# Eleven products of 128 rows for twelve of 112 in the projections of an attention kernel

## The chip, the cores and the metric

The kernel runs on one core of a Trainium2 chip. The metric is the device time of one execution in microseconds. A core has a matrix engine (PE, with its weight load PEld), three engines for vector work (DVE, ACT, POOL), a queue engine (SP) that here issues most of the transfers, and 16 DMA engines.

## What is computed

The output is the concatenation of two independent parts, each of 2048 rows by 448 columns, in fp32.

```
# part A: a state-space convolution, per feature
dt = exp(log_dt); A = -exp(log_A_real) + 1j*A_imag; C = (C_real + 1j*C_imag)*dt[:,None]
K = 2*einsum("dn,dnl->dl", C, exp((A*dt[:,None])[:,:,None]*arange(L))).real
a = irfft(rfft(u_t, 2L) * rfft(K, 2L))[..., :L] transposed + u * D_skip
# part B: attention with 16 heads of 28 features
q, k, v = split(x @ wqkv)               # x: 2048 x 448, wqkv: 448 x 1344
p = softmax(q k^T * 28**-0.5)
b = (p v) @ wo
```

The change touches the product x @ wqkv alone.

## The kernel before

The kernel runs in two stages. The first, about 190 us of the profiled execution, computes q, k and v and stores them in DRAM. Beside it, it builds the starting values ("seeds") of the state-space kernel for eight groups of features, in tiles called tri, sg, qhat and x_e, which end in the DRAM tensors sd. Then follow the row maxima of the first unit of attention, and from about 232 us on the main loop: 16 units of 16 steps with scores, exponentials and p v, in whose gaps the work of part A is placed.

In the first stage x comes in four blocks of 512 rows (c = 0 to 3, load_x). `transposes` (L464) turns a block into four slices of features by 512 rows with PE and splits each slice into a high part xh, rounded to fp32r by ACT, and the remainder xl, which DVE subtracts. The weights are split in the same way when the kernel starts: w_g with i = 0 and 1 (kept in the tile khat until the keys need it) for q and k, and vh and vl for v. A product of full precision is then taken as three products in fp32r, xh with the high weights, xh with the remainder of the weights, and xl with the high weights. Four slices of CK = 112 features make twelve products that accumulate in one PSUM tile:

```
for k in range(NCK):
    for i, x_ in ((0, xh), (1, xh), (0, xl)):
        nc.tensor.matmul(pp, w_g[:, i, s, k, g]..., x_[k], start=n == 0, stop=n == 3 * NCK - 1)
```

`qk_proj` (L474) is such a job for one block, for q or k (s = 0 or 1) and for one group of four heads, with 512 columns; `v_proj` (L509) one for 128 rows of v, with 448 columns. A block has eight jobs of the first kind and four of the second; in the last block the v jobs come first. The PSUM tiles of the jobs (pm) come from a ring of three banks. Each job ends in an evacuation by ACT and DVE (the tiles hl, vst, in the last block xn), and for keys also in kb and dhl, from where SP stores the results.

The weights come in through `wns`, four tiles of 112 rows. x blocks lie in xn, tiles of 512 columns of which 448 are used.

Around the change the order of the instructions is not written by hand: in this stage a scheduler in the build orders each engine's instructions by its own estimate of when they can start, from the program order of the jobs and of the seeds' slots (PW, SP and SH set how these are interleaved). The seeds' steps on ACT alone hold a fixed order among themselves. From the main loop on, instructions are kept in program order. All instructions are recorded by one helper, so that the profile gives line 75 for nearly all of them, and groups are told apart by their tiles.

Of the kernel before, what the change touches and what calls it, by code (L numbers as in the profile page):

```python
# [8 lines left out]
F32 = mybir.dt.float32  # L9
F32R = mybir.dt.float32r  # L10
I32 = mybir.dt.int32
AF = mybir.ActivationFunctionType
ALU = mybir.AluOpType
# [5 lines left out]
D = 448  # L19

H = 16
DH = 28
G = 4
HG = H // G
CQ = 512
NQ = L // CQ
NK = L // 128
CK = 112
NCK = D // CK
SCALE = DH ** -0.5  # L30
NU = G * NQ
NS = NU * NK
# [9 lines left out]
SGB, XB, XL = 2, 5, 4  # L42
# [48 lines left out]
def body(ctx, tc, a, out):  # L91
    nc = Engines(tc)
    nc.kept = KEPT["p"]
    x, wqkv, wo, u_a = a["B_x"][0], a["B_wqkv"], a["B_wo"], a["A_u"][0]
    out = out[0]

    def pool(stack, name, bufs=1, space=None, side=None):
        kw = {} if space is None else {"space": space}
        if side:
            kw["side"] = side  # L100
        return stack.enter_context(tc.tile_pool(name=name, bufs=bufs, reuse_waits="tile", **kw))
# [23 lines left out]
    def w_tile():  # L125

        n_ring[0] += 1
        return ps_w[0].tile([128, CQ], F32, name=f"pm{n_ring[0] % ps_w[1]}")
# [5 lines left out]
    k0_t = k0_p.tile([128, HG, L], F32R, name="khat")  # L134
# [91 lines left out]
    with ExitStack() as st:  # L226
# [3 lines left out]
        x_p = pool(xst, "x_p")  # L230
        y_p = pool(wst, "y_p", side="right")
        ps_w[0] = pool(st, "ps_w", 1, PSUM)
        ps_t = pool(st, "ps_t", 2, PSUM)
# [3 lines left out]
        xns = {}  # L237

        def load_x(c):
            xs = x[c * CQ:(c + 1) * CQ, :].rearrange("(t p) d -> p t d", p=128)  # L240
            for h in range(2):
                xns[c, h] = y_p.tile([128, 2, CQ], F32, name="xn", bufs=3)[:, :, :D]
                nc.sync.dma_start(xns[c, h], xs[:, 2 * h:2 * h + 2, :])

        first = lambda o: (o // 4) * DF + (o % 4) * (JF // 4)
        nats = {}
# [43 lines left out]
        def turn_dt():  # L290
            dt_ps = ps_t.tile([128, CQ], F32, name="pt")[:PO, :NO]
            nc.tensor.transpose(dt_ps, dt_o, ident[:NO, :NO])
            for i, f in enumerate((1.0, 0.15915494309189535, 2.0, -2.0, -1.0)):
                nc.vector.tensor_scalar(dt_all[:, i, :], dt_ps, f, None, op0=ALU.mult)

        load_x(0)
        w_g = k0_t[:CK].rearrange("p g (i s k h e) -> p i s k g h e", i=2, s=2, k=NCK, h=HG)
        vh = y_p.tile([CK, NCK, D], F32R, name="vh")
        vl = y_p.tile([CK, NCK, D], F32R, name="vl")
        nc.gpsimd.memset(k0_t[:CK].rearrange("p g (n e) -> p (g n) e", e=32)[:, :, DH:].bitcast(F32), 0.0)  # L300
        vst = [x_p.tile([128, H, 32], F32, name=f"vst{i}") for i in range(2)]
        for t in vst:
            nc.gpsimd.memset(t[:, :, DH:DH + 1], 1.0)
# [1 line left out]
        wns = []  # L305
        for i in range(2):
            wn = t_p.tile([128, 3, LV, BO * 16], F32, name="tri", bufs=2).rearrange("p t k h -> p (t k h)")
            wn = wn[:CK, :2 * 3 * D].rearrange("p (k s d) -> p k s d", k=2, s=3)
            wns += [wn[:, 0], wn[:, 1]]
        for k in range(NCK):  # L310
            nc.sync.dma_start(wns[k], wqkv[k * CK:(k + 1) * CK, :].rearrange("p (s d) -> p s d", s=3))
        pw2 = s_p.tile([128, LV], F32, name="pw2")
        nc.sync.dma_start(pw2, a["pw2"])
        nc.sync.dma_start(kones, a["kones"])
# [1 line left out]
        nc.sync.dma_start(w1, a["w1"])  # L316
        for k in range(NCK):
            for s in (1, 0):
# [143 lines left out]
        xh, xl = {}, {}  # L462

        def transposes(c):  # L464
            for k in range(NCK):
                pt = ps_t.tile([128, CQ], F32, name="pt")[:CK]
                for t in range(4):
                    nc.tensor.transpose(pt[:, t * 128:(t + 1) * 128], xns[c, t // 2][:, t % 2, k * CK:(k + 1) * CK], ident)
                xh[k] = x_p.tile([CK, CQ], F32R, name="xh", bufs=XB)
                xl[k] = x_p.tile([CK, CQ], F32R, name="xl", bufs=XL)  # L470
                nc.scalar.activation(xh[k], pt, AF.Copy)
                nc.vector.tensor_tensor(xl[k], pt, xh[k].bitcast(F32), ALU.subtract)

        def qk_proj(c, s, g):  # L474
            pp = w_tile()
            n = 0
            for k in range(NCK):
                for i, x_ in ((0, xh), (1, xh), (0, xl)):
                    nc.tensor.matmul(pp, w_g[:, i, s, k, g].rearrange("p h e -> p (h e)"), x_[k],
                                     start=n == 0, stop=n == 3 * NCK - 1)  # L480
                    n += 1

            def evac():
                if c == NQ - 1 and s == 0:
                    hl = y_p.tile([128, 2, CQ], F32, name="xn", bufs=3).bitcast(F32R)
                else:
                    hl = x_p.tile([128, 2, CQ], F32R, name="hl", bufs=3)
                th, tl = hl[:, 0], hl[:, 1]
                if s == 1:
                    nc.scalar.activation(th, pp, AF.Identity, bias=kones)  # L490
                    nc.vector.scalar_tensor_tensor(tl, pp, kones, th.bitcast(F32), op0=ALU.add, op1=ALU.subtract)
                else:
                    nc.scalar.activation(th, pp, AF.Copy)
                    nc.vector.tensor_tensor(tl, pp, th.bitcast(F32), ALU.subtract)
                if s == 1 and c < 2:
                    HC = CQ // 2
                    kb = y_p.tile([128, HC], F32, name="kb")
                    dhl = y_p.tile([128, 2, HC], F32R, name="dhl")
                    dh, dl = dhl[:, 0], dhl[:, 1]
                    nc.scalar.activation(kb, pp[:, HC:], AF.Copy)  # L500
                    nc.vector.tensor_tensor(kb, pp[:, :HC], kb, ALU.subtract)
                    nc.scalar.activation(dh, kb, AF.Copy)
                    nc.gpsimd.tensor_tensor(dl, kb, dh.bitcast(F32), ALU.subtract)
                    nc.sync.dma_start(kd_d[g][:, :, c * HC:(c + 1) * HC].rearrange("i p l -> p i l"), dhl.bitcast(F32))
                nc.sync.dma_start((k_d[g][:, :, c * CQ:(c + 1) * CQ] if s == 1 else q_d[g][c]).rearrange("i p l -> p i l"),
                                  hl.bitcast(F32))
            return evac

        def v_proj(c, t):  # L509
            pp = w_tile()  # L510
            n = 0
            ts = slice(t * 128, (t + 1) * 128)
            for k in range(NCK):
                for w_, x_ in ((vh, xh), (vl, xh), (vh, xl)):
                    nc.tensor.matmul(pp[:, :D], x_[k][:, ts], w_[:, k, :], start=n == 0, stop=n == 3 * NCK - 1)
                    n += 1

            def evac():
                vs = vst[t % 2]
                nc.scalar.activation(vs[:, :, :DH], pp[:, :D].rearrange("p (h e) -> p h e", e=DH), AF.Copy)  # L520
                nc.sync.dma_start(v_d[c][:, :, t], vs.rearrange("p (g h) e -> p g (h e)", g=G))
            return evac

        work = []
        for c in range(NQ):
            jobs = [lambda c=c, s=s, g=g: qk_proj(c, s, g) for g in range(G) for s in (1, 0)]
            v_jobs = [lambda c=c, t=t: v_proj(c, t) for t in range(4)]
            jobs = v_jobs + jobs if c == NQ - 1 else jobs + v_jobs
            jobs[0] = (lambda c, f: lambda: (transposes(c), f())[1])(c, jobs[0])
            if c + 1 < NQ:  # L530
                jobs[1] = (lambda c, f: lambda: (load_x(c + 1), f())[1])(c, jobs[1])
            work += jobs
# [572 lines left out]
    s = NS  # L1105
# [63 lines left out]
```

## Time and profile before

| what | us |
|---|---|
| median of three runs | 1278.88 |
| these runs | 1276.07 to 1279.31 |
| the profiled execution | 1278.37 |
| its span, first to last instruction | 1276.6 |
| PE busy in the span | 1223.9 |
| ACT busy | 967.5 |
| DVE busy | 923.0 |
| POOL busy | 846.2 |

The span is the time between the first and the last instruction on the core; the time of the execution also holds what lies around it. A busy PE is not a PE at its peak, since the ends of its pipelined products are modelled; the distance between the starts of two products tells its pace. Stretches of the stage are given in microseconds from the start of the span.

### The profile page before, as it was taken

What the parts mean: (1) busy time and instruction counts of PE and PEld (TensorE: products, weight loads), DVE (VectorE), ACT (ScalarE), POOL (GpSimd) and SP (SyncE); (2) the same over time, 40 slices, a digit from 0 to 9 for tenths busy, and PEclk for the clock granted to TensorE, in tenths of its full rate; (3) what the DMA queues carried; (4) which work ended last, traced back from release to release, by engine and by line L of the source; (5) the groups of instructions that cost most, each with busy time, mean ns of one, the idle gap of its engine ahead of it and who ended that gap; (6) DMA issues with size and microseconds to landing.
All of it is one profiled execution on the core that took longest, in us unless ns stands there. A gap on an engine that the chain in (4) does not pass through costs nothing.

```text
span 1276.6 us, 33328 instructions
## 1 busy us (share of the span) xinstructions
PE 1223.9 (96%) x12641; PEld 699.3 (55%) x12641; DVE 923.0 (72%) x2106; ACT 967.5 (76%) x2162; POOL 846.2 (66%) x728
## 2 busy tenths in 40 slices
PE   7789887999999999999999999999999999999997
PEld 5667664555555555555555555555555545544433
DVE  6788866877777877877788888888897645645111
ACT  6878765788888888888878888888887666656452
POOL 2666750897788888878599999989995222324321
PEclk9889999899999999999999999999999999999999
DMA  7768699446564645375633133422324533657666
GB/s 216 244 223 288 233 304 346 113 93 186 160 149 113 168 119 168 113 235 167 176 94 104 49 88 97 154 81 71 88 54 156 179 131 135 204 170 228 198 170 167
DMA packets 200089, 205.36 MB, mean 161 GB/s; under 512 B 95992, under 2 KB 158520, under 8 KB 197880
## 3 DMA queue, kind: packets, MB, share of 16 engines
q1 hardware_dynamic: 199400, 202.63, 52.6%
q8 instruction: 100, 1.64, 0.5%
q10 hardware_dynamic: 528, 0.59, 0.2%
q14 instruction: 61, 0.50, 0.1%
HBM read 120.73 MB, written 82.18 MB: 159 GB/s over the span
## 4 chain that ended last, share of the span: by engine, by line
PE 75%; DVE 8%; POOL 6%; ACT 4%; issue 3%; DMA 3%; SPq 0%; ACTq 0%; POOLq 0%; DVEq 0%
PE pm L75 43%; PE pss L75 16%; PE po L75 16%; POOL e L75 2%; DVE tri L75 1%; ACT rl L75 1%; POOL qhat L75 1%; DVE mx L75 1%; DVE sg L75 1%; POOL eu L75 1%; ACT tri L75 1%; DVE px L75 1%; DVE qhat L75 1%; DVE hl L75 1%; DMA sd<-qhat 1%
## 5 line engine op out<-in xcount | busy, mean ns | idle before, releaser
L75 ACT ACTIVATE p<-pss 128x512 f32<-128x512 f32 x1024 | 561.0, 610 | 112.5 <-PE pss L75 107.2
L75 PE MATMUL pss<-qhat,khat 128*128 128x512 f32 x1024 | 403.2, 400 | 1.5 <-ACT p L75 1.4
L75 DVE TENSOR_REDUCE mx<-pm 128x1 f32<-128x512 f32 x480 | 308.6, 684 | 109.1 <-PE pm L75 107.2
L75 PE MATMUL pm<-khat,qhat 128*128 128x512 f32 x749 | 325.9, 438 | 6.4 <-ACT rl L75 4.2
L75 POOL TENSOR_TENSOR e<-e,sdb 128x256 f32<-128x256 f32 x168 | 201.8, 1201 | 110.6 <-ACT e L75 101.2
L75 PE MATMUL po<-p,v 128*32 128x512 f32 x2048 | 269.1, 594 | 0.0
L75 POOL TENSOR_TENSOR e<-e,eu 128x256 f32<-128x256 f32 x168 | 248.2, 1477 | 13.2
L75 PEld LDWEIGHTS pm<-khat,qhat 128*128 128x128 f32 x749 | 141.0, 189 | 201.9 <-ACT p L75 47.8
L75 DVE CUSTOM_DVE_ANT_0 rl<-pm,rl 128x512 f32<-128x512 f32 x259 | 178.3, 689 | 72.1 <-ACT rl L75 69.1
L75 PEld LDWEIGHTS pss<-qhat,khat 128*128 128x128 f32 x1024 | 190.6, 189 | 46.7 <-issue 10.8
L75 POOL TENSOR_TENSOR eu<-e,sdb 128x256 f32<-128x256 f32 x168 | 201.9, 1202 | 0.0
L75 POOL TENSOR_TENSOR p<-pr,pr 64x448 f32<-64x448 f32 x64 | 73.2, 1144 | 158.2 <-PE pm L75 132.8
L75 ACT ACTIVATE rl<-pm 128x512 f32<-128x512 f32 x259 | 156.6, 606 | 14.0 <-PE pm L75 8.4
L75 DVE TENSOR_TENSOR g<-g,zg 128x128 f32<-128x128 f32 x392 | 162.2, 414 | 3.4
L75 PE MATMUL pm<-kdif,qhat 128*128 128x512 f32 x249 | 100.5, 403 | 4.3 <-DVE xn L75 2.4
L75 PE MATMUL pm<-xh,khat 112*128 112x512 f32 x256 | 87.3, 425 | 4.9 <-DVE hl L75 1.8
L75 DVE TENSOR_TENSOR zg<-g,zg 128x128 f32<-128x128 f32 x224 | 88.0, 393 | 5.1
L75 PEld LDWEIGHTS pm<-e,g 128*32 128x32 f32 x3584 | 57.2, 109 | 43.4 <-issue 17.1
L75 DVE TENSOR_TENSOR pr<-pm,ub 128x448 f32<-128x448 f32 x64 | 37.0, 620 | 56.4 <-PE pm L75 42.0
L75 PE MATMUL pm<-e,g 128*32 128x64 f32 x3584 | 73.0, 222 | 1.8 <-POOL e L75 1.8
L75 ACT ACTIVATE y<-pm 128x448 f32<-128x448 f32 x48 | 26.5, 553 | 58.2 <-PE pm L75 36.2
L75 ACT ACTIVATE ub<-pm 128x224 f32<-128x224 f32 (+1 forms) x96 | 38.8, 449 | 39.7 <-PE pm L75 37.3
(134 smaller groups left out, 1461.8 us busy)
## 6 DMA issues: line engine op xcount, KB each, us to landing
sdb<-sd SPq DMA_DIRECT2D x55, 336.0 KB
qhat<-q SPq DMA_DIRECT2D x64, 256.0 KB
khat<-k SPq DMA_DIRECT2D x64, 256.0 KB
sd<-sg SPq DMA_DIRECT2D x8, 1456.0 KB
k<-hl SPq DMA_DIRECT2D x16, 512.0 KB
mw<-in_mw SPq DMA_DIRECT2D x16, 512.0 KB
sd<-qhat SPq DMA_DIRECT2D x8, 896.0 KB
yu_d<-ub SPq DMA_DIRECT2D x64, 112.0 KB
```

The lines of the kernel that those rows point to most:

```text
L75: i = f(*args, **kw)
```

## The change

The 448 features are cut into three slices of 128 and a last one of 64. For that last slice x is loaded twice, so that the transposed slice holds the 64 features in rows 0 to 63 and again in rows 64 to 127. ACT rounds all 128 rows; DVE then overwrites the lower 64 rows with the remainder. The weights of the last slice are loaded twice as well. One product of 128 rows thus does for the last slice what two did (high part and remainder of x with the high weights), and a second takes both with the remainder of the weights. Three slices of three products and one of two make eleven. The x tiles get a second load of 64 columns for each half block, the last weight slice two loads of 64 rows, and memsets, casts and transposes cover 128 rows.

```diff
-CK = 112
-NCK = D // CK
+CK = 128
+NCK = 4
+TL = D - 3 * CK
...
             for h in range(2):
-                xns[c, h] = y_p.tile([128, 2, CQ], F32, name="xn", bufs=3)[:, :, :D]
-                nc.sync.dma_start(xns[c, h], xs[:, 2 * h:2 * h + 2, :])
+                xns[c, h] = y_p.tile([128, 2, CQ], F32, name="xn", bufs=3)
+                for d, n, at in ((0, D, 0), (D - TL, TL, D)):
+                    nc.sync.dma_start(xns[c, h][:, :, at:at + n], xs[:, 2 * h:2 * h + 2, d:d + n])
...
         for k in range(NCK):
-            nc.sync.dma_start(wns[k], wqkv[k * CK:(k + 1) * CK, :].rearrange("p (s d) -> p s d", s=3))
+            for p in range(1 if k < NCK - 1 else 2):
+                n = CK if k < NCK - 1 else TL
+                nc.sync.dma_start(wns[k][p * TL:p * TL + n], wqkv[k * CK:k * CK + n, :].rearrange("p (s d) -> p s d", s=3))
...
             for k in range(NCK):
-                pt = ps_t.tile([128, CQ], F32, name="pt")[:CK]
+                pt = ps_t.tile([128, CQ], F32, name="pt")
...
                 xh[k] = x_p.tile([CK, CQ], F32R, name="xh", bufs=XB)
-                xl[k] = x_p.tile([CK, CQ], F32R, name="xl", bufs=XL)
                 nc.scalar.activation(xh[k], pt, AF.Copy)
-                nc.vector.tensor_tensor(xl[k], pt, xh[k].bitcast(F32), ALU.subtract)
+                if k < NCK - 1:
+                    xl[k] = x_p.tile([CK, CQ], F32R, name="xl", bufs=XL)
+                    nc.vector.tensor_tensor(xl[k], pt, xh[k].bitcast(F32), ALU.subtract)
+                else:
+                    nc.vector.tensor_tensor(xh[k][TL:], pt[TL:], xh[k][TL:].bitcast(F32), ALU.subtract)
...
-                for i, x_ in ((0, xh), (1, xh), (0, xl)):
+                for i, x_ in ((0, xh), (1, xh), (0, xl))[:3 if k < NCK - 1 else 2]:
                     nc.tensor.matmul(pp, w_g[:, i, s, k, g].rearrange("p h e -> p (h e)"), x_[k],
-                                     start=n == 0, stop=n == 3 * NCK - 1)
+                                     start=n == 0, stop=n == 3 * NCK - 2)
...
-                for w_, x_ in ((vh, xh), (vl, xh), (vh, xl)):
-                    nc.tensor.matmul(pp[:, :D], x_[k][:, ts], w_[:, k, :], start=n == 0, stop=n == 3 * NCK - 1)
+                for w_, x_ in ((vh, xh), (vl, xh), (vh, xl))[:3 if k < NCK - 1 else 2]:
+                    nc.tensor.matmul(pp[:, :D], x_[k][:, ts], w_[:, k, :], start=n == 0, stop=n == 3 * NCK - 2)
```

More of the change, by code (lines that the diff above doesn't have):

```diff
@@ L296, in body @@
         load_x(0)
-        w_g = k0_t[:CK].rearrange("p g (i s k h e) -> p i s k g h e", i=2, s=2, k=NCK, h=HG)
+        w_g = k0_t.rearrange("p g (i s k h e) -> p i s k g h e", i=2, s=2, k=NCK, h=HG)
         vh = y_p.tile([CK, NCK, D], F32R, name="vh")
         vl = y_p.tile([CK, NCK, D], F32R, name="vl")
-        nc.gpsimd.memset(k0_t[:CK].rearrange("p g (n e) -> p (g n) e", e=32)[:, :, DH:].bitcast(F32), 0.0)
+        nc.gpsimd.memset(k0_t.rearrange("p g (n e) -> p (g n) e", e=32)[:, :, DH:].bitcast(F32), 0.0)
         vst = [x_p.tile([128, H, 32], F32, name=f"vst{i}") for i in range(2)]
@@ L307, in body @@
             wn = t_p.tile([128, 3, LV, BO * 16], F32, name="tri", bufs=2).rearrange("p t k h -> p (t k h)")
-            wn = wn[:CK, :2 * 3 * D].rearrange("p (k s d) -> p k s d", k=2, s=3)
+            wn = wn[:, :2 * 3 * D].rearrange("p (k s d) -> p k s d", k=2, s=3)
             wns += [wn[:, 0], wn[:, 1]]
         for k in range(NCK):
-            nc.sync.dma_start(wns[k], wqkv[k * CK:(k + 1) * CK, :].rearrange("p (s d) -> p s d", s=3))
+            for p in range(1 if k < NCK - 1 else 2):
+                n = CK if k < NCK - 1 else TL
+                nc.sync.dma_start(wns[k][p * TL:p * TL + n], wqkv[k * CK:k * CK + n, :].rearrange("p (s d) -> p s d", s=3))
         pw2 = s_p.tile([128, LV], F32, name="pw2")
```

## The prediction

> **What bounds the kernel now.** I read the page first, then the busy table cut at the places where the work changes, then the chain of waits by stage, then the timeline of PE, ACT and SP inside the first stage. The table's columns are stretch, length, and busy microseconds with instruction counts of PE, weight load, DVE, ACT and POOL, then granted clock, DMA share and GB/s.
>
> ```profile
> PE 1223.9 (96%) x12641; PEld 699.3 (55%) x12641; DVE 923.0 (72%) x2106; ACT 967.5 (76%) x2162; POOL 846.2 (66%) x728
> PE   7789887999999999999999999999999999999997
> ```
>
> ```profile
> 0.00:10.99 10.99, 3.27 (x12) 2.09 (x13) 5.20 (x24) 3.38 (x6) 2.66 (x16) 1.00 0.81 211
> 10.99:40.41 29.42, 28.12 (x126) 21.51 (x126) 19.20 (x37) 23.95 (x55) 11.89 (x15) 1.00 0.76 221
> 40.41:50.67 10.26, 9.88 (x48) 8.93 (x48) 10.26 (x20) 9.33 (x26) 6.08 (x5) 1.00 0.71 249
> 50.67:89.03 38.36, 31.66 (x128) 23.99 (x129) 30.18 (x59) 29.47 (x78) 25.87 (x35) 0.82 0.76 260
> 89.03:105.30 16.27, 13.70 (x57) 11.77 (x56) 11.56 (x22) 12.17 (x30) 9.77 (x12) 0.79 0.52 179
> 105.30:133.50 28.20, 25.68 (x119) 19.73 (x117) 27.96 (x51) 25.68 (x65) 19.60 (x23) 1.00 0.89 304
> 133.50:146.40 12.90, 11.71 (x61) 9.88 (x61) 11.99 (x23) 11.28 (x33) 9.48 (x14) 1.00 0.73 257
> 146.40:160.54 14.14, 12.12 (x63) 9.70 (x63) 11.25 (x24) 10.75 (x22) 7.95 (x11) 1.00 0.59 179
> 160.54:187.00 26.46, 24.75 (x98) 19.02 (x96) 18.51 (x36) 16.74 (x40) 15.61 (x20) 0.94 0.89 294
> 187.00:216.60 29.60, 24.14 (x80) 14.23 (x79) 21.22 (x62) 20.63 (x38) 1.65 (x2) 0.94 0.95 343
> 232.00:1276.60 1044.60, 1028.06 (x11832) 552.39 (x11831) 745.71 (x1732) 798.42 (x1766) 731.43 (x573) 1.00 0.48 138
> ```
>
> From 232 us on PE is busy 1028.06 of 1044.60 us: the main loop is bound by PE, and the change touches nothing in it. In the built order of both programs every engine's sequence from the end of the projections on is the same, instruction for instruction. So all that can move lies before 187 us, the stage of projections, which shares its engines with the building of the state-space factors ("seeds": tri, sg and qhat tiles). There PE is nearly full in the first stretch (28.12 of 29.42) and the last (24.75 of 26.46); between them DVE is as full or fuller (10.26 of 10.26, 27.96 of 28.20). The chain of waits says the same. Its three lines below are for 9 to 188 us, 40.4 to 89 us, and 160.5 to 188 us:
>
> ```profile
> by line: PE pm L75 15.3%; DVE tri L75 9.8%; issue 9.1%; POOL qhat L75 7.8%; DVE sg L75 6.7%; ACT tri L75 5.5%; DVE px L75 5.2%; DVE qhat L75 5.2%; DVE hl L75 4.8%; DMA sd<-qhat 4.6%; DMA tri<-in_B_wqkv 4.3%; POOL x_e L75 3.2%; SPq L75 2.2%;
> ...
> by line: POOL qhat L75 22.6%; DMA sd<-qhat 17.0%; POOL x_e L75 11.8%; DVE tri L75 11.0%; DVE qhat L75 8.4%; issue 6.0%; DVE hl L75 5.2%; DVE px L75 3.2%; DVE xl L75 2.4%; ACT tri L75 2.2%; DVE pn L75 2.2%; POOL gz L75 2.1%; POOL tri L75 1.6
> ...
> by line: PE pm L75 37.3%; SPq L75 14.1%; DVE sg L75 13.6%; DMA kdif<-kd 13.1%; issue 7.8%; DVE px L75 5.5%; DVE hl L75 5.2%; ACT hl L75 2.5%; DVE qhat L75 1.0%; ACT sg L75 0.3%; DVE tri L75 0.2%; ACTq L75 0.1%; DVEq L75 0.1%
> ```
>
> PE's products carry 15.3% of the chain over the whole stage and 37.3% of its last part; from 40.4 to 89 us they are not among the chain's largest shares at all, which belong to the seeds.
>
> **The products taken away.** Each of the 32 jobs for q and k (four blocks of rows, eight jobs) and each of the 16 for v issues eleven products for twelve. Starts on PE's timeline give the pace: start, length, what, count, and the wait before in brackets.
>
> ```profile
> 142.11 0.36 PE L75 MATMUL pm<-vl,xh 112*128 112x448 f32 x1
> 142.31 0.36 PE L75 MATMUL pm<-vh,xl 112*128 112x448 f32 x1
> ...
> 177.67 0.62 PE L75 MATMUL pm<-xh,khat 112*128 112x512 f32 x2
> 178.13 0.40 PE L75 MATMUL pm<-xl,khat 112*128 112x512 f32 x1
> 178.37 0.62 PE L75 MATMUL pm<-xh,khat 112*128 112x512 f32 x2
> ```
>
> Three products of 512 columns take 178.37 - 177.67 = 0.70 us, 0.233 each; one of 448 takes 0.200. All of it is 32 x 0.233 + 16 x 0.200 = 10.7 us, the upper end. The lower end comes from the chain: 15.3% of 179 us is 27.4 us, and a twelfth of that 2.3 us. Between them I count by stretch. The first is PE-bound and loses eight products, 1.87 us; so is the last, another 1.87 us. In the v jobs at 94 us PE was the chain too:
>
> ```profile
> 94.23 8.00 PE pm L75 x24
> ```
>
> At that place the 24 become 22, and two products at the pace shown further down (0.373) are 0.75 us. Elsewhere I cost the saving at nothing: DVE and the seeds hide it. Sum: 4.5 us off the path. If that cover were gone, all 10.7 would count.
>
> **Taller tiles.** Contraction over 128 rows instead of 112, weight casts of 128 rows, and the subtraction into 64 rows of xh that replaces one of four xl per block keep their instruction counts.
>
> ```profile
> L75 DVE TENSOR_TENSOR xl<-pt,xh 112x512 fp32r<-112x512 f32 x16 | 10.8, 684 | 2.2 <-ACT xh L75 2.2
> L75 DVE TENSOR_TENSOR hl<-pm,hl 128x512 fp32r<-128x512 f32 x12 | 8.2, 682 | 1.2 <-ACT hl L75 1.2
> ```
>
> 684 ns on 112 rows and 682 on 128: rows don't set the time, columns do. So 0, bounded by a gain of 4 x 0.68 = 2.7 us on DVE if 64 rows were free, which the row speaks against. The new wait is that both products of the last slice need DVE's subtraction, where only the third did; behind them on PE stand the next jobs, but this slice is the last of four, so the subtraction has the other nine products (2.1 us) for cover. Without it: 0.7 us per block.
>
> **More to load at the start.** Each x load gets a second one of 64 columns, the last weight slice is loaded twice over 64 rows. These stand ahead of and between the weights on SP's queue:
>
> ```profile
> 1.20 0.98 SPq L75 DMA_DIRECT2D xn<-in_B_x  x2
> 2.54 5.36 SPq L75 DMA_DIRECT2D tri<-in_B_wqkv  x4
> ...
> 10.27 1.04 ACT L75 ACTIVATE khat<-tri 112x448 fp32r<-112x448 f32 x2 [1.30 <-DMA tri<-in_B_wqkv]
> 16.36 1.05 ACT L75 ACTIVATE khat<-tri 112x448 fp32r<-112x448 f32 x2 [1.62 <-DMA tri<-in_B_wqkv]
> ```
>
> Two further issues are 0.98 us. In bytes: two pieces of 65.5 KB, and 86 KB more for each weight slice. At the 211 GB/s of the first 11 us the first slice lands (131 + 86)/211 = 1.0 us later, the third (131 + 258)/211 = 1.8 us. ACT waited for both, and PE for ACT. The built order adds a further step: on DVE seed 0's first operations (three short ones and one of 1.44 us) now stand before the last weight remainder, where they stood behind it and two evacuations.
>
> ```profile
> L75 DVE TENSOR_TENSOR tri<-pn,pw 128x1232 f32<-128x1232 f32 x8 | 11.5, 1437 | 0.0
> ```
>
> That bounds the start between 1.0 and 1.8 + 2.3 = 4.1 us later; I take 2.0, near the landing of the third slice, because the seeds gain what this DVE step costs. The six later x pieces are 6 x 0.49 us of SP time, queued before loads for seeds and stores of k and q; x is loaded a block ahead and SP mostly waits for engines, so 0; uncovered, about 1 us per block.
>
> The page "DMA: Bandwidth & Descriptors" of the Trainium skill, section Specifications, asks for at least 512 B per transfer to reach line rate, and the new x pieces are 256 B per row; no such transfer is in a row here. As an estimate, at half rate the first two pieces would cost 0.6 us more, and the sum would be 1276.5.
>
> **Sum.** 1278.37 us is the profiled execution (its span is 1276.6), half a microsecond under the median of 1278.88. 1278.37 - 4.5 + 2.0 = 1275.9, rounded to **1276.0**. With 2.3 to 6.2 us off the path and 1.0 to 4.1 on it, this case spans 1273.2 to 1280.2.
>
> **Rivals.** *PE sets the pace everywhere.* For: the largest busy time of the stage, in nearly every stretch. Against: the chain between 40 and 160 us. Then 10.7 comes off and 1.0 to 2.0 is added: 1269.
>
> *The seeds set the pace to the end.* For: seed 7's transposes still have 121 products behind them in the new order (120 before), so the tail after them doesn't shrink. Then only the start counts: 1280.4.
>
> *Freed time becomes waits that halve the clock*, the slower side. These are the pace and the waits:
>
> ```profile
> 40.41 0.47 PE L75 MATMUL pm<-vh,xh 112*128 112x448 f32 x1 [0.93 <-DVE hl L75]
> 40.72 0.37 PE L75 MATMUL pm<-vl,xh 112*128 112x448 f32 x1
> ...
> 94.23 0.74 PE L75 MATMUL pm<-vh,xh 112*128 112x448 f32 x1 [2.57 <-DVE hl L75]
> 96.27 0.57 PE L75 MATMUL pm<-vh,xh 112*128 112x448 f32 x1
> 96.64 0.57 PE L75 MATMUL pm<-vl,xh 112*128 112x448 f32 x1
> 100.64 0.36 PE L75 MATMUL pm<-vh,xl 112*128 112x448 f32 x1
> ...
> 133.52 0.47 PE L75 MATMUL pm<-vh,xh 112*128 112x448 f32 x1 [1.27 <-DVE hl L75]
> 133.83 0.36 PE L75 MATMUL pm<-vl,xh 112*128 112x448 f32 x1
> ...
> 168.29 0.85 PE L75 MATMUL pm<-xh,khat 112*128 112x512 f32 x2 [1.59 <-DVE hl L75]
> 169.37 1.05 PE L75 MATMUL pm<-xh,khat 112*128 112x512 f32 x2
> 170.65 1.05 PE L75 MATMUL pm<-xh,khat 112*128 112x512 f32 x2
> ```
>
> After waits of 0.93 and 1.27 us the pace stayed full. After 1.59 it was 1.28/3 = 0.427 per product of 512 for about 3.6 us, after 2.57 it was 0.373 per product of 448 until 100.4. So a wait of 1.59 us decides. PE would reach the waits at 40 and 133 us up to 1.87 us sooner (eight products) while DVE is as late as now: 2.8 and 3.1 us, over that point. Each drop then costs 17 x (0.373 - 0.200) = 2.9 us. Two of them, the late start, and no gain but the last stretch's 1.87: 1278.4 + 5.8 + 2.0 - 1.9 = 1284.3. Against it: at both places DVE set the pace, so a slow PE has room.
>
> The page "TensorE: Matmul & The Clock Gate" of the Trainium skill, section What's actually happening, halves the clock after an idle window of about 3.4 us. By that rule neither wait would drop it, and this rival would fall back to the forecast; the trace agrees on the half (0.427 against 0.233) but not on the length, since 1.59 us was followed by it.
>
> **Chances.** About 0.3% (3.8 us) is what a measurement can tell from no change: 1275.0 to 1282.7. The forecast's case has 0.50, of which 0.18 lies under 1275.0; PE everywhere 0.22; seeds to the end 0.06; clock drops 0.22. Faster 0.18 + 0.22 = 0.40, same 0.32 + 0.06 = 0.38, slower 0.22. The range from 1268.5 to 1284.5 takes in all four; left out is what the first and the last would exceed.
>
> **What would show it.** In the new profile: 48 fewer products; the third weight cast near 18.2 us for 16.36; the last k and q products ending about 2.5 us before 187, and the main loop's first pss as much earlier than now, with a loop of the same length. If the stage ends 8 us earlier, PE set the pace; if new half-speed stretches follow 40 or 133 us, the last rival; if the main loop's own length changes, the whole account is wrong.

## The result, and the profile after

The changed kernel takes 1280.38 us (median of 20 runs, 1279.42 to 1283.25) beside 1279.15 for the kernel before on the same chip (20 runs, 1276.07 to 1280.0): ratio 1.0016, 95% interval 1.001 to 1.0023. By the ratio that is 0.16%, some 2.0 us, slower (the two medians lie 1.2 us apart); inside the 0.3% called no change, but on the other side of the forecast of 1276.0, which meant 2.9 us less. The profiled execution took 1280.57 us with a span of 1278.8. Of the runs below, one of `a_actq` (6491.52 us) and one of `a_copy_twelve_xl3` (1681.43 us) were slow and are left out of every median and ratio.

The products are gone as announced. First two lines of the page after, busy time and the span in 40 slices:

```profile
PE 1217.4 (95%) x12593; PEld 692.5 (54%) x12593; DVE 924.3 (72%) x2106; ACT 966.6 (76%) x2162; POOL 846.3 (66%) x728
PE   6979788999999999999999999999999999999997
```

48 products fewer (12,641 to 12,593), 6.5 us less PE time, and a span 2.2 us longer. Where, the first product of the main loop tells; the tile view of pss, before and then after, gives its first and last start:

```profile
L75 PE MATMUL pss<-qhat,khat x1024: 387/396/628, 228.6 to 1251.2; 128*128 128x512 f32 x171
```

```profile
L76 PE MATMUL pss<-qhat,khat x1024: 387/396/505, 231.2 to 1253.2; 128*128 128x512 f32 x171
```

The loop begins 2.6 us later; from there to the end of the span it takes 1278.8 - 231.2 = 1047.6 us, where it took 1276.6 - 228.6 = 1048.0. All that moved lies before the loop, but not all of it in the stage of the projections. PE's first q or k product starts at 12.55 us where it started at 10.99. The last one, before and then after, ends 1.0 us later:

```profile
186.53 0.40 PE L75 MATMUL pm<-xl,khat 112*128 112x512 f32 x1
```

```profile
187.29 0.62 PE L76 MATMUL pm<-xh,khat 128*128 128x512 f32 x2
```

The other 1.6 us come between that end and the first pss (43.3 us for 41.7), where the row maxima stand. Each of these profiles is one execution, and the kernel before alone ranges over 3.9 us, so parts of this size are not certain. The table of stretches after (columns as in the prediction):

```profile
12.55:44.46 31.91, 28.80 (x112) 21.29 (x113) 22.10 (x43) 24.02 (x58) 13.43 (x16) 0.89 0.61 183
53.70:86.80 33.10, 27.43 (x118) 20.85 (x116) 27.56 (x52) 27.25 (x70) 19.70 (x28) 0.90 0.82 278
104.40:132.70 28.30, 24.43 (x112) 18.61 (x113) 26.11 (x47) 25.34 (x62) 17.75 (x22) 1.00 1.00 334
147.90:165.19 17.29, 13.08 (x52) 9.79 (x52) 14.68 (x28) 15.10 (x35) 11.32 (x14) 0.80 0.68 222
165.19:188.20 23.01, 21.29 (x89) 16.55 (x89) 13.34 (x27) 11.85 (x26) 10.54 (x17) 1.00 0.86 278
234.00:1278.80 1044.80, 1028.14 (x11832) 552.37 (x11831) 745.47 (x1733) 798.49 (x1766) 732.63 (x574) 1.00 0.47 138
```

The first stretch, which the prediction had 1.87 us shorter, grew from 29.42 us at a granted clock of 1.00 to 31.91 at 0.89. The last stretch of k and q products did shrink, from 26.46 us with 96 of them to 23.01 with 88. But it starts at 165.19 where it started at 160.54: all it won was lost before it. PE's timeline after shows how, with waits in brackets:

```profile
24.39 1.04 PE L76 MATMUL pm<-xh,khat 128*128 128x512 f32 x3 [1.93 <-DVE khat L76]
27.05 2.08 PE L76 MATMUL pm<-xh,khat 128*128 128x512 f32 x4 [1.19 <-DVE hl L76]
...
94.88 0.74 PE L76 MATMUL pm<-vh,xh 128*128 128x448 f32 x1 [5.19 <-DVE kb L76]
95.42 0.57 PE L76 MATMUL pm<-vl,xh 128*128 128x448 f32 x1
...
98.03 0.36 PE L76 MATMUL pm<-vh,xl 128*128 128x448 f32 x1
```

The wait of 2.57 us at 94.23 has become one of 5.19 us at 94.88. PE was free for the v jobs 2.0 us sooner (94.88 - 5.19 = 89.69 for 94.23 - 2.57 = 91.66) and began them 0.65 us later. SP's timeline holds what the change adds; these are all x loads after:

```profile
1.19 2.26 SPq L76 DMA_DIRECT2D xn<-in_B_x  x4
12.78 6.43 SPq L76 DMA_DIRECT2D xn<-in_B_x  x4
59.84 5.19 SPq L76 DMA_DIRECT2D xn<-in_B_x  x4
110.97 4.70 SPq L76 DMA_DIRECT2D xn<-in_B_x  x4
```

Each line is one block, from its first issue to the end of its last: 18.6 us together, with the waits between the issues in it. Two of the same lines before:

```profile
16.30 0.95 SPq L75 DMA_DIRECT2D xn<-in_B_x  x2
...
111.62 1.16 SPq L75 DMA_DIRECT2D xn<-in_B_x  x2
```

Two issues of the second block were 0.95 us and are now four in 6.43; two of the last were 1.16 and are now four in 4.70. The tile view of xn (least, median and longest issue in ns) takes the issues alone: all x loads before, all after, and the second block after. Below it stands what SP waited for after, from 12 to 20 us (us, times, longest):

```profile
L75 SPq DMA_DIRECT2D xn<-in_B_x x8: 378/436/626, 1.2 to 112.3; - x8
```

```profile
L76 SPq DMA_DIRECT2D xn<-in_B_x x16: 367/607/1987, 1.2 to 115.1; - x16
```

```profile
L76 SPq DMA_DIRECT2D xn<-in_B_x x4: 367/373/379, 12.8 to 18.8; - x4
```

```profile
SPq L76 <- DMA tri<-in_B_wqkv: 5.6, 4, 3.0
```

So most of the 6.43 us is SP waiting for weight tiles to land. Added up, the x issues themselves took 3.7 us before and 13.1 after.

### The profile page after: what moved, and what is told of

The parts are those of the page before. It is cut to its first block, busy times and chain, and to the rows that moved or that the text cites. A ratio compares the mean times of both kernels' runs of the same rounds, so it can differ in the third digit from the quotient of the medians.

```text
span 1278.8 us, 33240 instructions
## 1 busy us (share of the span) xinstructions
PE 1217.4 (95%) x12593; PEld 692.5 (54%) x12593; DVE 924.3 (72%) x2106; ACT 966.6 (76%) x2162; POOL 846.3 (66%) x728
## 2 busy tenths in 40 slices
DMA packets 202343, 206.21 MB, mean 161 GB/s; under 512 B 98184, under 2 KB 160712, under 8 KB 200136
## 4 chain that ended last, share of the span: by engine, by line
PE 77%; DVE 8%; ACT 4%; POOL 4%; DMA 3%; issue 3%; ACTq 0%; SPq 0%; POOLq 0%; DVEq 0%
PE pm L76 44%; PE pss L76 17%; PE po L76 16%; DVE tri L76 1%; DVE sg L76 1%; DVE mx L76 1%; ACT rl L76 1%; ACT tri L76 1%; POOL e L76 1%; DVE hl L76 1%; POOL qhat L76 1%; DVE px L76 1%; POOL p L76 1%; DVE qhat L76 1%; DMA tri<-in_B_wqkv 1%
## 5 line engine op out<-in xcount | busy, mean ns | idle before, releaser
L76 ACT ACTIVATE rl<-pm 128x512 f32<-128x512 f32 x259 | 156.5, 605 | 15.2 <-PE pm L76 8.7
L76 PE MATMUL pm<-xh,khat 128*128 128x512 f32 x256 | 84.8, 425 | 11.6 <-DVE hl L76 7.6
```

The source lines that it names most:

```text
L76: i = f(*args, **kw)
```

## The experiments

Two theories of the products: in the **seeds theory** (S) the state-space factors (tri, sg, qhat on DVE, ACT, POOL) pace the stage, and a product less only makes PE wait longer; in the **products theory** they count in part, as predicted. Each kernel was timed in five rounds beside the kernel before; ratios are to that.

**The products alone.** `b_eleven` is the kernel before without the last slice's product with xl, and with nothing added (that part of the sum is left out). `a_twelve` is the changed kernel with the second product of the last slice issued twice.

```diff
 # b_eleven (in v_proj alike; stop follows)
-                for i, x_ in ((0, xh), (1, xh), (0, xl)):
+                for i, x_ in ((0, xh), (1, xh), (0, xl))[:3 if k < NCK - 1 else 2]:
 # a_twelve (in v_proj alike; stop follows)
-                for i, x_ in ((0, xh), (1, xh), (0, xl))[:3 if k < NCK - 1 else 2]:
+                for i, x_ in ((0, xh), (1, xh), (0, xl) if k < NCK - 1 else (1, xh)):
```

> The kernel before with one product fewer per job: the last slice's remainder of x is left out of the sum (that part of the result is missing), its loads, tiles and weight casts stay as before. So it has the saving on PE and none of the added loads. If the seeds set the pace of the stage (theory S), nothing is gained: 1277.5 to 1280.5. If the added loads at the start ate a real gain (theory L), the gain shows here without them: 1273 to 1276, and 1268.5 to 1270 if PE sets the pace everywhere.

> The changed kernel with the twelfth product put back: the second product of the last slice is issued twice, so a small term counts twice. Loads and tiles are those of the change. Theory S: the 10.7 us of products are hidden as they were before, 1279.5 to 1282.5. Theory L: products count on the path, so it gets slower by what the change won, 1284 to 1291.

Measured: 1278.18 us, ratio 0.9998 (0.9989 to 1.0006); and 1280.58 us, 1.0021 (1.0008 to 1.0035), against the changed kernel's 1.0016. Taking 48 products from the old kernel gains nothing that can be measured, and giving 48 back to the new one costs nothing that can be measured. The same stretch before and in `b_eleven` shows where the time went:

```profile
10.99:187.00 176.01, 157.60 (x694) 124.53 (x694) 140.92 (x265) 139.36 (x342) 106.25 (x133) 0.93 0.76 251
```

```profile
10.99:187.00 176.01, 150.46 (x642) 119.19 (x642) 137.93 (x263) 138.83 (x343) 104.64 (x132) 0.89 0.75 249
```

PE works 7.1 us less in it and idles as much more, and the first pss starts at 229.0 us, no earlier than before (228.6).

**Who sets the pace.** `b_four` is the kernel before with only the first of three products per slice (two thirds of the projections' work left out). In `b_noseeds` and `a_noseeds` the seeds are built for one group and stored for all eight (seven groups' factors left out).

```diff
 # b_four (in v_proj alike; stop follows)
-                for i, x_ in ((0, xh), (1, xh), (0, xl)):
+                for i, x_ in ((0, xh),):
 # b_noseeds, a_noseeds (in seeds(o), whose q is shared by all groups)
+            if o:
+                return [[] for _ in range(11)] + [[put_g], [put_e]]
```

> The kernel before with only the first of the three products of each slice: 8 of 12 products a job are left out, 32 x 8 x 0.233 + 16 x 8 x 0.200 = 85 us of TensorE time. If the products pace the stage in the share that the prediction took (4.5 of 10.7), some 36 us less, 1242. If the seeds pace it (seeds theory), under 8 us less, 1270 or more.

> The kernel before with the seeds built for one group of features only; the other seven groups store the first group's tiles (so part A is wrong, the stores and the main loop stay). Their input loads and all their steps on PE, DVE, ACT and POOL are gone. Theory S: the stage of projections gets much shorter, since PE's own work there is about 140 us of 190: the time falls by 25 to 45 us. If PE or the loads set the pace, it falls by less than 10 us.

> The changed kernel with the same seven groups of seeds left out. Theory S: with the seeds gone PE sets the pace, and the product saved shows: 6 to 10 us under the same cut of the kernel before. Theory L: the late start remains, and it lies within 2 us of that one. Theory C (freed time becomes waits that halve the clock): also within 2 us or above.

`b_four`: 1269.19 us, 0.9925 (0.9913 to 0.9938). 85 us of products left out bring 9.6 us (0.75% of 1278.5), 0.11 us for each, a little past the 8 us that the seeds theory allowed and far from the 36 of the other. Its table of stretches, and the line of its chain of waits from 12 to 165 us:

```profile
0.00:60.00 60.00, 33.85 (x112) 24.02 (x113) 42.34 (x93) 43.34 (x102) 27.78 (x49) 0.81 0.74 227
60.00:120.00 60.00, 37.63 (x119) 26.61 (x119) 55.26 (x106) 54.40 (x143) 41.22 (x53) 0.62 0.81 277
120.00:182.00 62.00, 39.38 (x100) 25.34 (x100) 49.00 (x95) 46.48 (x113) 39.56 (x50) 0.55 0.83 280
```

```profile
by line: ACT tri L75 11.9%; DVE tri L75 10.0%; issue 9.7%; PE pm L75 7.3%; DMA nat<-in_A_C_real 6.4%; DVE sg L75 5.8%; DVE hl L75 5.2%; DVE px L75 4.9%; ACT L75 4.2%; DVE qhat L75 4.1%; DMA xn<-in_B_x 3.7%; ACT sg L75 3.5%; ACT nat L75 2.5%
```

PE idles 40% of the time, and runs at a clock of 0.62 and 0.55, and still the stage hardly shortens: in the second of these stretches DVE is busy 55.26 and ACT 54.40 of 60 us. `b_noseeds` is the counterpart: 1245.34 us, 0.9744 (0.9731 to 0.9756), 33 us gained. Its stretch from 60 to 120 us and its chain from 12 to 165 us:

```profile
60.00:120.00 60.00, 59.66 (x278) 49.74 (x277) 14.72 (x22) 17.33 (x33) 2.94 (x4) 1.00 0.92 322
```

```profile
by line: PE pm L75 77.4%; DMA v<-vst 4.5%; PE pt L75 2.9%; issue 2.4%; POOL qhat L75 1.4%; ACT hl L75 1.3%; DVE qhat L75 1.1%; DVE px L75 0.9%; DVE hl L75 0.9%; ACT tri L75 0.8%; ACT rl L75 0.8%; ACT vst L75 0.7%; POOL gz L75 0.7%; SPq L75 
```

There PE is full and its products carry 77.4% of the chain; in the changed kernel, same window, they carry 7.2%:

```profile
by line: issue 11.6%; DVE tri L76 9.4%; PE pm L76 7.2%; DVE sg L76 6.6%; POOL qhat L76 6.3%; ACT tri L76 6.1%; DVE hl L76 5.5%; DMA tri<-in_B_wqkv 5.1%; DVE qhat L76 4.9%; DVE px L76 4.8%; DMA xn<-in_B_x 3.8%; DMA sd<-qhat 3.5%; POOL tri L7
```

The ends show it too: the last product of q and k and the seeds' last step on DVE (tile sg), before and in `b_four`:

```profile
186.53 0.40 PE L75 MATMUL pm<-xl,khat 112*128 112x512 f32 x1
187.17 0.56 DVE L75 TENSOR_TENSOR sg<-sg,px 128x224 f32<-128x224 f32 x1
```

```profile
166.79 3.75 PE L75 MATMUL pm<-xh,khat 112*128 112x512 f32 x8 [0.28 <-DVE hl L75]
176.31 0.56 DVE L75 TENSOR_TENSOR sg<-sg,px 128x224 f32<-128x224 f32 x1
```

The products end 16.4 us earlier in `b_four`, the seeds 10.9, and the main loop starts 9.4 us earlier (219.2 for 228.6): it follows the seeds, not the products. The seeds theory holds for the whole kernel. But it missed on `a_noseeds`: 1251.95 us, 0.979 (0.9774 to 0.9806), 6.6 us behind `b_noseeds` where it should have led. So the change has a price of its own.

**The price: the x loads.** `b_xloads` and `bn_xloads` are the kernel before, whole and with the seeds' cut, with the changed kernel's second x loads into columns that nothing reads. `a_copy` and `an_copy` are the changed kernel, whole and cut, with a copy on POOL in their place.

```diff
 # b_xloads, bn_xloads
-                nc.sync.dma_start(xns[c, h], xs[:, 2 * h:2 * h + 2, :])
+                for d, n, at in ((0, D, 0), (D - 64, 64, D)):
+                    nc.sync.dma_start(xns[c, h][:, :, at:at + n], xs[:, 2 * h:2 * h + 2, d:d + n])
 # a_copy, an_copy
-                for d, n, at in ((0, D, 0), (D - TL, TL, D)):
-                    nc.sync.dma_start(xns[c, h][:, :, at:at + n], xs[:, 2 * h:2 * h + 2, d:d + n])
+                nc.sync.dma_start(xns[c, h][:, :, :D], xs[:, 2 * h:2 * h + 2, :])
+                nc.gpsimd.tensor_copy(xns[c, h][:, :, D:], xns[c, h][:, :, D - TL:D])
```

> The kernel before, with the changed kernel's second x load of 64 columns (256 B a row) put behind each of its eight x loads; what it brings is read by nothing. If the loads carry the cost of the change (loads theory), about 1280.5 us, some 2 us over before. If the cost comes from the taller tiles and the order that they bring at the start (order theory), within 0.5 us of before, 1278.5.

> The changed kernel, whole, with the second x load replaced by a copy of the 64 columns on GpSimd. Loads theory: 1278 or a little below, level with before, since the seeds set the pace from there. Order theory: 1280 to 1281, as the changed kernel.

> The same unread x loads in the kernel before with the seeds of seven groups left out (1245.3 us without the loads). Loads theory: they make up most of the 6.6 us by which the changed kernel was behind with the same cut, so 1250 to 1252. Order theory: 1245 to 1246.

> The changed kernel with the seeds of seven groups left out (1251.95 us), the second x load replaced by a copy of the 64 columns on GpSimd. Loads theory: the products saved show at last, 1238 to 1245. Order theory: stays at 1250 to 1252.

`b_xloads`: 1279.83 us, 1.0017 (1.0008 to 1.0026): the loads, with nothing else of the change, cost the old kernel all that the change costs. `a_copy`: 1276.42 us, 0.9987 (0.9977 to 0.9996): without them the changed kernel is a little ahead of the old one. With the seeds cut the loads theory failed: `bn_xloads` 1247.75 us, 0.9765 (0.9751 to 0.9778), 2.4 us over `b_noseeds`, lies between the two forecasts, and `an_copy` 1251.8 us, 0.9798 (0.9785 to 0.9812), no better than `a_noseeds`, came out as the order theory had it. What puts the changed kernel behind there was not settled. From 12 to 165 us PE's products waited 15.2 us in `a_noseeds` and 7.6 in `b_noseeds`; the longest of these waits, 5.2 us, was for an evacuation of v, and ACT stood 6.0 us there before a store of v had landed. The granted clock was lower as well (0.88 from 12 to 40 us, 1.00 in `b_noseeds`), and of the three theories of its forecast only the clock's "within 2 us or above" allows a result so far behind.

**Which of them.** `a_copy_first` copies only for the first block (c == 0), `a_copy_later` only for the other three (c > 0); the rest is loaded.

```diff
-                for d, n, at in ((0, D, 0), (D - TL, TL, D)):
+                xcopy = c == 0     # a_copy_later: c > 0
+                for d, n, at in ((0, D, 0), (D - TL, TL, D))[:1 if xcopy else 2]:
...
+                if xcopy:
+                    nc.gpsimd.tensor_copy(xns[c, h][:, :, D:], xns[c, h][:, :, D - TL:D])
```

> The changed kernel with the second x loads of the first block (two of eight) replaced by copies on GpSimd. If the price of the loads lies at the start (start theory, the prediction's +2.0 us with the later six at nothing), 1276.5 or so, as with all eight replaced. If it lies in the later blocks, 1280 to 1281.

> The mirror of it: the second x loads of the three later blocks (six of eight) replaced by copies, the first block's kept. Start theory: 1280 to 1281, no gain. Later-blocks theory: 1276.5 or so.

1278.63 us, 1.0002 (0.9993 to 1.0011), and 1277.55 us, 0.9994 (0.9985 to 1.0003). Against the changed kernel's 1.0016 the first block's two pieces are worth 0.0014, 1.8 us, the later six 0.0022, 2.8 us; all eight 0.0029, 3.7 us. The intervals are some 0.001 to either side, so how the price is shared is not certain; neither theory alone fits.

**Queue or transfer.** `a_poolq` and `a_actq` are the changed kernel with the second loads issued from POOL's and from ACT's queue.

```diff
+                    q_ = nc.gpsimd if at else nc.sync     # a_actq: nc.scalar
-                    nc.sync.dma_start(xns[c, h][:, :, at:at + n], xs[:, 2 * h:2 * h + 2, d:d + n])
+                    q_.dma_start(xns[c, h][:, :, at:at + n], xs[:, 2 * h:2 * h + 2, d:d + n])
```

> The changed kernel with its eight second x loads issued from GpSimd's queue in place of SP's; they move the same bytes in the same rows of 256 B. If the price of these loads is the time that their issues hold SP's queue (queue theory; the x issues took 18.6 us there for about 4 in the kernel before), it goes as with the copies: 1276 to 1277.5. If it is the transfer itself (transfer theory), 1280 to 1281.

> The same with ACT's queue in place of SP's. ACT is a busy engine in this stage (25 us of 28 in places), so an issue there takes its time from the evacuations. Queue theory: 1276 to 1279 by what ACT loses. Transfer theory: 1280 to 1282.

1276.96 us, 0.9988 (0.9979 to 0.9996), and 1274.75 us, 0.9971 (0.9959 to 0.9982). The page's count of packets tells what is moved; first after, then `a_actq`:

```profile
DMA packets 202343, 206.21 MB, mean 161 GB/s; under 512 B 98184, under 2 KB 160712, under 8 KB 200136
```

```profile
DMA packets 202344, 206.22 MB, mean 161 GB/s; under 512 B 98184, under 2 KB 160712, under 8 KB 200136
```

The same 98,184 small packets, and 4.5 parts in a thousand apart; and beside `a_copy` (0.9987), which moves none of the second pieces, neither version is slower. So it is not the moving of the 256-byte rows. (`a_poolq` moved them in 2,048 small packets fewer, so it says less. The profiled execution of `a_actq`, 1281.15 us, is the slowest of its seven; its trace can't show the gain.) The x loads on SP's queue in `b_xloads`, then in `a_copy`, by the tile view:

```profile
L75 SPq DMA_DIRECT2D xn<-in_B_x x16: 367/538/1433, 1.2 to 110.4; - x16
```

```profile
L76 SPq DMA_DIRECT2D xn<-in_B_x x8: 378/642/1440, 1.2 to 109.9; - x8
```

Added up, 11.9 us of issues against 6.6. What is shown is that these loads cost the whole kernel time on SP's queue, and none that can be measured off it: the queue theory's forecast came out for `a_poolq`, and `a_actq` is faster than its own of 1276 to 1279. The theory's reason, that the loads hold up the seeds' loads and the stores of k, q and v behind them, is argued and not shown, because a rival was not tested. The scheduler orders the stage anew when the loads move. Taken in order of start up to 185 us, DVE and ACT run the same instructions in `b_copy` as in the kernel before, and in `a_poolq` as in `a_copy` (so that pair tells what moving the pieces alone costs: 0.9988 and 0.9987, nothing). But `b_xloads` leaves the order of the kernel before at DVE's 20th and ACT's 5th instruction, and `a_copy` leaves that of the changed kernel at the same two places. Whether time on SP's queue or the other order costs the 2 us, no run here tells: none held the order and moved the loads off SP's queue.

`a_actq`, which computes all of the reference, is the fastest version measured that keeps eleven products, though its interval overlaps those of `a_poolq` and `a_copy`; by the ratios it beats the kernel before by 0.29% and the changed one by 0.45%.

**Where the rest comes from.** Without the price the changed kernel leads the old one, though products gain nothing. Four more runs asked why: `a_copy_twelve` (copies, and twelve products a job), `b_copy` (the kernel before with the copies, unread), `a_copy_twelve_xl3` (the first of these with three buffers for xl) and `a_copy_pw34` (copies, and the jobs spread over 34 steps).

```diff
 # a_copy_twelve: the diffs of a_copy and a_twelve together
 # b_copy, on the kernel before
+                nc.gpsimd.tensor_copy(xns[c, h][:, :, D:], xns[c, h][:, :, D - 64:D])
 # a_copy_twelve_xl3, on a_copy_twelve
-SGB, XB, XL = 2, 5, 4
+SGB, XB, XL = 2, 5, 3
 # a_copy_pw34, on a_copy
-SP, SH, PW, E3 = 4, 3, 37, 8
+SP, SH, PW, E3 = 4, 3, 34, 8
```

> The changed kernel with all eight second x loads replaced by copies (1276.4 us) and the second product of the last slice issued twice, so twelve products a job again. If what it wins over the kernel before is the saved products, 1278 to 1279, level with before. If products are hidden behind the seeds (seeds theory), 1276 to 1277, and the gain has another source.

> The kernel before, whole, with eight copies on GpSimd of the last 64 columns of each x tile into columns that nothing reads. If the copies (or the order of work that they bring) are what made the versions with copies faster than the kernel before, 1275 to 1276.5. If it is the taller slices, 1278 to 1279, or a little above for GpSimd's time.

> The changed kernel with copies for the second x loads and twelve products a job (1274.7 us), its low parts given three buffers in place of four. A block of the changed kernel makes three low parts (the kernel before makes four for four buffers), so the fourth buffer lets the next block begin early. If that is the gain (buffer theory), it goes: 1278 to 1279. If not, 1274 to 1275.5.

> The changed kernel with copies for the second x loads (1276.4 us), its projection jobs spread over 34 of the planner's steps in place of 37. If the seeds pace the stage and TensorE has room beside them, the jobs that stand alone at its end move in beside the seeds: 1272 to 1275. If TensorE or the queues are full there, 1276.4 or more.

1274.71 us, 0.9977 (0.9963 to 0.9991): again not the products. 1278.80 us, 1.0 (0.9989 to 1.0011): not the copies. 1274.66 us, 0.9972 (0.9962 to 0.9982): not the spare buffer. (`b_copy` and `a_copy_twelve_xl3` kept DVE's and ACT's order of the kernel that each is compared with, so these two are clean.) What is left is the slices of 128 rows and the order that the scheduler makes of them; which of these was not told apart. And 1276.78 us, 0.9989 (0.9979 to 0.9999): placing the jobs earlier gains nothing over `a_copy`. PE had room for them beside the seeds; the last product and the seeds' last step in `a_copy_pw34` are

```profile
175.67 0.63 PE L76 MATMUL pm<-xh,khat 128*128 128x512 f32 x2
182.74 0.55 DVE L76 TENSOR_TENSOR sg<-sg,px 128x224 f32<-128x224 f32 x1
```

In `a_copy` the products end at 182.2 us, 5.9 us later, the seeds' last step starts at 182.98, and the main loop at 225.6 us for 227.6 here. The earlier products gained nothing because the seeds ended no earlier.

## Why the prediction was wrong, point by point

- **The main loop and all behind 188 us**: right for the loop, the same length within 0.4 us. The stretch between the last product and the loop, taken as unchanged, was 1.6 us longer in these profiles.
- **4.5 us of products off the path**: this step failed. It took a stretch as bound by PE because PE was busy 28.12 of 29.42 us there. (Its sentence that DVE is as full or fuller in between holds for three of the six stretches there.) Without the products PE's time became waiting: 7.1 us less work in `b_eleven`, and no earlier end. In the changed kernel the first stretch grew by 2.5 us where a gain of 1.87 was forecast, and the v jobs at 94 us waited 5.19 us for 2.57. `b_eleven` bounds the term to between a gain of 1.4 us and a loss of 0.8, and by the rate of `b_four` it would be 10.7 x 0.11 = 1.2 us. The 6.2 us at the upper end of the forecast's own case are worked out nowhere. Even the lower end of 2.3 us, a twelfth of PE's share of the chain, was too much: a chain that runs through an engine for 15.3% does not shorten by a cut on it when another chain stands close behind.
- **Taller tiles at nothing**: no run shows a cost. In the whole kernel they may even be the small gain left open above.
- **The start, +2.0 us**: the size came out, 1.8 us by `a_copy_first`, though the way named fits only in part, and 1.8 is a difference of two ratios with some 0.001 of doubt in each. The first weight cast did come later, by 1.57 us (10.27 before; 1.0 was forecast), and with it PE's first product, 12.55 for 10.99. `b_xloads`, which has the loads alone, starts its products at 12.82, and `a_copy`, which has none, at 10.23. But the third weight cast, which was to come near 18.2 us, is where it was (16.36). ACT's timeline after:

```profile
11.84 1.03 ACT L76 ACTIVATE khat<-tri 128x448 fp32r<-128x448 f32 x2
...
16.16 1.05 ACT L76 ACTIVATE khat<-tri 128x448 fp32r<-128x448 f32 x2 [0.55 <-DMA tri<-in_B_wqkv]
```

  The step of DVE's new order did come; DVE's timeline after has the last weight remainder behind the seed's work, at 23.72 where it stood at 19.31, and PE waited for it (1.93 us, above). So this wait is the order's doing, not that of the missing products:

```profile
22.36 1.44 DVE L76 TENSOR_TENSOR tri<-pn,pw 128x1232 f32<-128x1232 f32 x1
23.72 1.15 DVE L76 TENSOR_TENSOR khat<-tri,khat 128x448 fp32r<-128x448 f32 x2
```

- **The six later pieces at nothing**: this failed as well. They were costed at 0.49 us of SP's time each, from two issues at the start when the queue was empty. In the stage an x issue took up to 1.99 us, a block with its waits 4.70 to 6.43 us, and `a_copy_later` puts the six at 2.8 us of the kernel's time. That SP "mostly waits for engines" was read as room; but behind these loads stand the seeds' loads, and the seeds set the pace. Whether it is that, or the scheduler's other order, stays open.
- **The rival that was right**: seeds to the end, with 0.06 and 1280.4 us, against 1280.38 measured. The chain between 40 and 160 us, quoted for it, and DVE's 27.96 of 28.20 us should have given it most of the chance. Its own price was still right in part by luck: it charged the start with 2.0 us and the later pieces with nothing, and it counted from 1278.37 us where the kernel before had a median of 1279.15 beside the changed one.
- **The clock rival**: the waits came, and half pace with them. At 94 us it was there before, and for longer; new is the granted clock of 0.89 in the first stretch. What that cost the changed kernel no run separates. `b_four` ran at 0.55 to 0.62 of the clock over two thirds of the stage and was 9.6 us faster, so half pace need not cost where the seeds set the pace.
- **The 256-byte rows**: the page "DMA: Bandwidth & Descriptors" of the Trainium skill, section Specifications, asks for 512 B to reach line rate. No run shows that this costs time here: with the same packets `a_actq` is the faster one. Small packets were nothing new either, though the prediction has none in its rows: the page before counts 95,992 under 512 B, the page after 98,184. The same page, section Issuing engines are not separate DMA queues, says that another issuing engine saves only the time of the issue, usually small beside the transfer. No run here shows that the time of the issue is all that was saved: the order of the stage changed as well. With both, another engine's queue saved the whole price of this change.

## What to carry to other kernels

An engine that is busy 95% of a stretch need not set its pace; before an edit on it is priced, cut far more of its work than the edit would (as `b_four` did) and see what the time does. Price a DMA that is added by the queue it is issued on, at the place where it stands, and by what waits behind it there, not by an issue in an empty queue. Where a scheduler orders the work, compare the orders too before the queue is blamed. If an added transfer is small and its queue feeds the stage's pace, give it another queue or copy on the chip.

## What was not expected of the hardware

One issue of an x load took SP between 0.37 and 1.99 us in the changed kernel. The added loads are not needed for the long ones: `a_copy`, which has none, goes up to 1.44 us, where the kernel before stays under 0.63. What it depends on was not tested. After the wait of 5.19 us the half pace (0.37 us for a product of 448) lasted from 94.88 to 98.03, 3.15 us. After the wait of 1.59 us in the prediction it lasted 3.6 us, and after that of 2.57 us, from 94.23 to 100.64 before, 6.4 us: a longer wait did not make a longer slow stretch. The page "TensorE: Matmul & The Clock Gate" of the Trainium skill, section What's actually happening, gives about 3.4 us of sustained work until the full clock; with 3.15 and 3.6 us the traces agree, with 6.4 us they do not.
